# A DeltaNet and SwiGLU kernel whose order of work is planned anew: other durations and another search

## The chip, the cores and the metric

The kernel runs on one core of a Trainium2 chip. The time is the device time of one execution in microseconds; the median of several runs counts. The five engines of the core work side by side, each through its own queue and in order: TensorE (PE; its weight loads are listed apart, as PEld), VectorE (DVE), ScalarE (ACT), GpSimd (POOL) and SyncE (SP), which here only issues DMA transfers. An engine that waits for another holds up everything queued behind the waiting instruction.

## The reference

```python
# deltanet: q, k, v are (4, 8, 768, 48), beta is (4, 8, 768); float32
k_n = k / (norm(k, axis=-1) + 1e-06)
state = zeros((B, H, D, D))
for t in range(S):
    y[:, :, t] = einsum('bhd,bhde->bhe', q[:, :, t], state)
    v_old = einsum('bhde,bhd->bhe', state, k_n[:, :, t])
    state = state + beta_t * einsum('bhd,bhe->bhde', k_n[:, :, t], v[:, :, t] - v_old)
x = y.transpose(0, 2, 1, 3).reshape(3072, 384)
# ffn: d_model 384, d_ff 1536
xn = x / sqrt(mean(x * x) + 1e-06) * rms_g
out = (silu(xn @ w_gate) * (xn @ w_val)) @ w_out
```

The weights arrive as 64-bit floats and are turned into float32 in the kernel.

## The kernel before

**Blocks.** The 768 time steps are cut into 12 blocks of 64. A block c holds all 32 sequences (batch times heads) and yields 256 rows for the FFN. For each block the kernel does four things.

- It reads k, forms its norms (L728 to L735: a Square on ACT, a sum on VectorE, a root on POOL by L731, 1/x on VectorE), turns k (L685, copies L697) and forms the scores of k with itself (L704).
- It inverts the block's triangular matrix. For blocks 0 and 1 (`prep16`) the matrix is taken apart into 16 by 16 pieces: L774/L776, a gather L848, the copy L862, the transpose L865, then pairs of instructions L903 and L909, each pair two columns on, then L924/L926, L929 and the scatter L936. For later blocks (`kscores`, `keep`, `invert`) the scores go through device memory (`dkk`): four writes by SP, two reads into `at`, then L1023, L1048 to L1058 and 15 pairs L1070 and L1076, a POOL copy L1096, and small transfers that spread the result (`dx`, `dxt`, `mt`, `x2bd`, `m1bd`).
- It runs the recurrence (`recur`): products of the state with k and q (L1199, L1210), the corrected values u (L1281 to L1355), q-scores times u (L1317), the update of the state (L1404, L1522), and the norm of the result: L1439, the Square L1445, the root on POOL (L1452 to L1455, in `root`), the scaling L1465, the turn L1483 and, on ACT, L1495, which writes x.
- It runs the FFN on x. Blocks 0 and 1 use plain products (`ffn_plain`: L1558 up, L1565/L1566, L1540 down). Later blocks use a scheme with fewer products (`ffn`: L1651 up, L1661 and L1663 collect, L1667, L1668; `down`: L1708, L1700, L1713, L1717).

**Weights.** The weights come in 18 pieces (`weights`), each read by one DMA of 768 KB into one of three buffers (two early ones elsewhere) and converted by five instructions: ACT L619, then VectorE L607, L610, L615, L639. Later VectorE forms sums of the weights (L1612, L1687).

**q.** For blocks from 2 on, q is read by 16 small transfers (`load`, issued through L487) and turned by one VectorE transpose (`square_turn`, L715).

**What sets the order.** Nothing in the code's order of calls does. Every step is an `Op` with an engine, a planned duration, a priority and the keys it reads and writes; `Plan.run` decides the order of all engines before an instruction is emitted. It does so with a list schedule (`forward`) over the planned durations: an engine takes the op that can start first, then the one with the lowest key. A DMA op takes a planned issue time on SP (`dur`) and then a share of one modelled transfer server (`work`). VectorE's next op may start 0.08 us before an op's planned end (`OVERLAP`). `run` repeats this: first ROUNDS[1] rounds, in which keys are set by a backward pass and shaken by a random generator with seed ROUNDS[0]; then one round for each number in MOVES, which is the seed of one shake that starts from the keys of the round before. The order with the earliest planned end is emitted. Where TensorE is planned to stand idle before 70 us, `fillers` sets dummy products (L1826) into the gap. PSUM's eight banks go from op to op as the plan frees them.

So a changed planned duration moves no instruction by itself. It changes what the plan takes to be early, and by that the order in all five queues.

Of the kernel before, what the change touches and what calls it, by code (L numbers as in the profile page):

```python
# [22 lines left out]
STRETCH = {"PE": 1.5, "ACT": 1.5, "DVE": 1.4, "POOL": 1.2, "SP": 1.0}  # L23
ENGINES = ("PE", "ACT", "DVE", "POOL", "SP")
OVERLAP = {"PE": 0.0, "ACT": 0.1, "DVE": 0.08, "POOL": 0.06, "SP": 0.0}
ROUNDS, MOVES = (8, 3), (8000067, 8000597, 8000948, 8001017, 8002724, 8006360, 8008220, 8019300, 8029128, 8041120, 8046040, 8061420, 8103060, 8171660, 8171980, 8172520, 8176051, 8186548, 8187777, 8188940, 8197021, 8197169, 8200311, 8221546, 8225628, 8270861, 8283640, 8284428, 8285760, 8285870, 8288410, 8295221, 8301729, 8305291, 8310247, 8324080, 8458740, 8499977, 8522895, 8527737, 8540674, 8542770, 8573880, 8576584, 8577340, 8579620, 8580620, 8594840, 8603040, 8637560, 8655411, 8656870, 8664720, 8672920, 8873930, 8885129, 8893086, 8956398, 8960108, 9314698, 9382016, 9442358, 9601943)
BLOCK, ASKED, LACKED = 256, 140, 193
REACT, TURN, LAND = 2.4, 3.45, 2.6
STICK = 1.0
# [315 lines left out]
def kernel(  # L345
# [17 lines left out]
    nc = tc.nc  # L363
# [21 lines left out]
    half = sbt("half", [128, 16])  # L385
# [23 lines left out]
    q2t = q2.rearrange("p x e -> p (x e)").rearrange("p (u g th e) -> p u g th e", u=8, g=2, th=2)  # L409
    q2k = [("q2", i) for i in range(16)]  # L410
# [19 lines left out]
    AK = [("acc", 0), ("acc", 1)]  # L430
# [17 lines left out]
    ms = sbt("ms", [128, 2, 2], 2)  # L448
    rs = sbt("rs", [128, 2], 2)
# [29 lines left out]
    P = Plan()  # L479
    V = lambda n: 0.13 + 0.0011 * n  # L480
    VF = lambda n: 0.13 + 0.0006 * n
    A = lambda n: 0.2 + 0.0008 * n
    G = lambda n: 0.15 + 0.0022 * n

    def dma(dst, src, prio, r=(), w=(), work=0.3, dur=0.5, eng="SP", after=0.0):
        queue = nc.scalar if eng == "ACT" else nc.sync
        op = P.add(eng, dur, lambda: queue.dma_start(out=dst, in_=src), prio, r, w, lat=0.7)  # L487
        op.dma, op.work, op.ready, op.port = True, work, after, False
        return op

# [2 lines left out]
    def due(c, lead):  # L493

        return (64.0 - min(lead, 64.0)) if c == 0 else (90.0 if c == 1 else 152.9 + PERIOD * (c - 2)) - lead
# [156 lines left out]
    def load(c, what):  # L652
        t0 = c * C
        pk, pq, pv = ((-5, 1, 12), (5, 29, 36))[c] if c < 2 else (due(c, 150), due(c, 99), due(c, 70))
        if "q" in what and c > 1:
            for d, eh, g, th in itertools.product(range(2), repeat=4):
                e0, e1 = 32 * eh, min(D, 32 * eh + 32)
                src = q.rearrange("b (yh a) t e -> a t (b yh) e", a=4)[2 * d + g, t0 + 32 * th : t0 + 32 * th + 32, :, e0:e1]
                r0 = 64 * d + 32 * eh
                dma(q2t[r0 : r0 + 32, :, g, th, 0 : e1 - e0], src, pq, w=[q2k[8 * d + 4 * eh + 2 * g + th]], work=0.33 if eh else 0.43, after=due(c, 85))  # L660
        for key, t, src, pr in (("k2", k2[c % NK], k, pk), ("q2", q2, q, pq)):
            for g in range(2):
                if key[0] not in what or key == "q2" and c > 1:
                    continue
                dst = t[64 * g : 64 * g + 64, :, 0:D]
                s = src.rearrange("b (y g) t e -> g t (b y) e", g=2)[g, t0 : t0 + C]
                op = dma(dst, s, pr, w=[(key, c % NK, g)] if key == "k2" else q2k[8 * g : 8 * g + 8], dur=0.7, work=1.18, eng="ACT" if c == 0 and (g or key == "q2") else "SP", after=((0.0, 1.4, 0.0), (5.0, 40, 0.0))[c]["kqv".index(key[0])] if c < 2 else 44.5)
                op.lat += LATE if c == 1 or key == "q2" else 1.2 if c == 0 else 0.0
        if "v" in what and c < 2:
            for g in range(2):  # L670
                s = v.rearrange("b (y g) t e -> g t (b y) e", g=2)[g, t0 : t0 + C]
                dma(vt[64 * g : 64 * g + 64], s, pv, w=[("v", g)], dur=0.7, work=1.18, after=30 if c else 8).lat += LATE
        elif "v" in what:
            for bb in range(2):
                s = v[2 * bb : 2 * bb + 2, :, t0 : t0 + C, :].rearrange("p h t e -> t (p h) e")
                dma(vt[64 * bb : 64 * bb + 64], s, pv, w=[("v", bb)], dur=0.85, work=1.18, after=due(c, 75))
# [106 lines left out]
    def prep16(c):  # L783
        pr = 8.0 if c == 1 else 0.0
        pd = pr + (1 if c else 0)
        pi = (1.0, 45.0)[c]
        i2, ikq = c, c
# [10 lines left out]
        psf = Group()  # L798
# [57 lines left out]
        ab = [("ab", c, n) for n in range(4)]  # L856
        ak = [("acc", c)]
# [15 lines left out]
                nc.scalar.copy(flat(side)[:, L * c : L * c + 33 * 15 + 1 : 33], share())  # L873

        P.add("ACT", 0.6, start, pd, r=["half"], w=ak)
        P.add("ACT", 0.4, start2, pd + 0.5, r=[psf], w=ak, last=psf)
        x, xkeys = x16[c], [("xs", c)]
        diag = a16[c].rearrange("p j t -> p (j t)")[:, 1 : 1 + 34 * 7 + 1 : 34]
        pair = x.rearrange("p i t -> p (i t)")[:, 0:128].rearrange("p (j k) -> p j k", k=L // 2)
# [17 lines left out]
        for j in range(0, L - 2, 2):  # L897
            n, m = j + 2, L - 2 - j

            def step(j=j, n=n, m=m):  # L900
                old, new, lo = (3, 0, 1) if j % 4 else (0, 3, 0)
                cols = slice(L * c + j + 2, L * c + L)
                nc.vector.tensor_tensor(  # L903
                    out=acc[:, 1:3, 0:n, cols].rearrange("p a i t -> p i a t"),
                    in0=sides[old][:, 0:n, j : j + 2, None].to_broadcast([128, n, 2, m]),
                    in1=a16[c][:, None, j : j + 2, j + 2 : L].to_broadcast([128, n, 2, m]),
                    op=ALU.mult,
                )
                nc.vector.tensor_reduce(  # L909
                    out=acc[:, new, 0:n, cols],  # L910
                    in_=acc[:, lo : lo + 3, 0:n, cols].rearrange("p a i t -> p i t a"),
                    axis=AXL.X,
                    op=ALU.add,
                )

            P.add("DVE", 0.47 + 0.0052 * n * m, step, pi, r=ab, w=ak)

        xflat = x.rearrange("p i t -> p (i t)")

# [5 lines left out]
                else:  # L925
                    nc.vector.tensor_copy(out=dst, in_=src)  # L926

        P.add("ACT" if c else "DVE", 0.97 if c else 0.55, spread, pi, r=ak, w=xkeys)
        P.add("DVE", V(256), lambda: nc.vector.transpose(out=turned[1], in_=xflat), pi, r=xkeys, w=["turn1"])  # L929
        psb = Group()  # L930

# [12 lines left out]
        for h in range(2):  # L944
            dst = dg[c][:, 8 * h : 8 * h + 8].rearrange("p x (n m) -> p x n m", n=4)
            src = lambda h=h: psb.t[:, 128 * h : 128 * h + 128].rearrange("p (x m) -> p x m", x=8)[:, :, None].to_broadcast([128, 8, 4, L])
            w = [("dg", c, h)] + (kkall if c else [])
# [62 lines left out]
    def invert(c):  # L1010
        pd = due(c, 110) + 1
# [3 lines left out]
        dkeys = [("dkk", c % 2, g, i) for g in range(2) for i in range(2)]  # L1015
        for par in range(2):
            dma(at_[64 * par : 64 * par + 64].rearrange("p j t -> p (j t)"),
                dk.rearrange("i g x j t -> (i g x) (j t)"), pd, r=dkeys, w=[("at", par)] + [(n_, p_, z) for n_ in ("ab",) for p_ in range(2) for z in range(4)] + [("xs", 0), ("xs", 1)], dur=0.56, work=0.95)
        bt = beta_b[:, c]
        bkeys = [("beta", i) for i in range(8)]  # L1020

# [14 lines left out]
                        bt[rows, par : W : 2],  # L1036
                    )

        P.add("ACT", 1.0, start, pd, r=["half"], w=AK)
        P.add("ACT", 0.9, start2, pd + 0.5, r=bkeys, w=AK)  # L1040


# [22 lines left out]
        for j in range(0, W - 2, 2):  # L1065
            n, m = j // 2 + 1, W - 2 - j

            def step(j=j, n=n, m=m):
                old, new, lo = (3, 0, 1) if j % 4 else (0, 3, 0)
                nc.vector.tensor_tensor(  # L1070
                    out=acc[:, 1:3, 0:n, j + 2 : W].rearrange("p a i t -> p i a t"),
                    in0=acc[:, old, 0:n, j : j + 2, None].to_broadcast([128, n, 2, m]),
                    in1=at_[:, None, j : j + 2, j + 2 : W].to_broadcast([128, n, 2, m]),
                    op=ALU.mult,
                )
                nc.vector.tensor_reduce(  # L1076
                    out=acc[:, new, 0:n, j + 2 : W],
                    in_=acc[:, lo : lo + 3, 0:n, j + 2 : W].rearrange("p a i t -> p i t a"),
                    axis=AXL.X,
                    op=ALU.add,  # L1080
                )

            P.add("DVE", 0.47 + 0.0052 * n * m, step, pi, r=[("at", 0), ("at", 1)], w=AK)

        def spread(dst, op, turn):
            for side in range(2):
# [90 lines left out]
    def recur(c):  # L1177
# [245 lines left out]
        for h in halves:  # L1423
            gy = groups(psy, h)

            if c == 0:
                p = h[0]
                for g in range(2):
                    P.add("ACT", A(192) + 0.15, lambda p=p, g=g: nc.scalar.activation(
                        out=xflat[:, 128 : 320], in_=psy[g, p].t[:, 192 * p : 192 * p + 192], func=ACTF.Square,  # L1430
                        scale=1.0 / math.sqrt(DM), accum_out=ms[i2][:, p, g : g + 1],
                    ), py, r=[psy[g, p]], w=[("x1", 1), ("ms", i2, p)], last=psy[g, p])
# [21 lines left out]
                    nc.gpsimd.tensor_scalar(out=ms[i2][:, cols, 0], in0=ms[i2][:, cols, 0], scalar1=ms[i2][:, h[0], 1:2], scalar2=1e-6, op0=ALU.add, op1=ALU.add)  # L1454
                nc.gpsimd.tensor_tensor(out=rs[i2][:, cols], in0=ms[i2][:, cols, 0], in1=mhalf[:, cols], op=ALU.pow)  # L1455

            P.add("POOL", 1.1, root, py, r=["half"], w=[(k_, i2, p) for p in h for k_ in ("ms", "rs")])
            if c == 0:
                p = h[0]
                P.add("DVE", V(128), lambda p=p: nc.vector.tensor_scalar(  # L1460
# [401 lines left out]
```

## Time and profile before

| what | us |
|---|---|
| runs | 670.78, 671.55, 674.18; median 671.55 |
| profiled execution, its own time | 673.21 |
| its span, first to last instruction | 671.5 |
| TensorE busy | 657.3 (98%) |
| VectorE busy | 577.0 (86%) |
| ACT busy | 298.2 (44%) |
| POOL busy | 88.5 (13%) |
| mean granted clock | 0.994 |

The page cuts the span into 40 slices of 16.8 us; a digit is the busy share of a slice in tenths. Rows of the trace name a line, an engine, an operation and its tiles; where idle time goes before a row, it stands in brackets with what ended it. A helper's line stands for all that call it: L487 is the line of all DMA issues.

| group | count | mean ns |
|---|---|---|
| L1651 PE (up products, blocks 2 to 11) | 2400 records | 276, 277 |
| L1708 PE (down products) | 360 records | 329 |
| L1661 DVE | 180 | 683 |
| L1070 and L1076 DVE (inversion pairs) | 150 and 150 | 351 and 472 |
| at<-dkk, 256 KB, issue to landing | 20 | 3.7 us |
| more<-w_gate, 768 KB, issue to landing | 6 | 7.6 us |

### The profile page before, as it was taken

How to read it: one execution, taken by the hardware profiler on the slowest of the kernel's cores; microseconds unless marked ns; L12 is line 12 of the kernel's file. 1: busy time of each engine (PE TensorE's matmuls, PEld its weight loads, DVE VectorE, ACT ScalarE, POOL GpSimd, SP SyncE). 2: the span in 40 equal slices, each digit the busy share in tenths (PEclk: the TensorE clock that was granted, in tenths of full speed). 3: DMA queues.
4: the chain of work that ended last, by engine and by line, in shares of the span. 5: the costliest groups of instructions: out<-in, count | busy, mean ns of one | idle time of the engine just before them, and what ended most of it. 6: DMA issues, size and time to landing. Idle time of an engine off the chain costs nothing.

```text
span 671.5 us, 23512 instructions
## 1 busy us (share of the span) xinstructions
PE 657.3 (98%) x10070; PEld 608.2 (91%) x10070; DVE 577.0 (86%) x1199; ACT 298.2 (44%) x685; POOL 88.5 (13%) x105
## 2 busy tenths in 40 slices
PE   9899989999999999999999999999999999999997
PEld 6788768787799999999999999999999999999997
DVE  6999889999999998997998898899998798457472
ACT  7554343454235455355345345345345354343241
POOL 4212211050300040040031030030040010000000
PEclk9999979999999999999999999999999999999999
DMA  9483666573325336345347456476346434102100
GB/s 233 125 221 108 135 166 167 91 146 75 48 63 79 63 84 107 57 99 91 54 123 109 76 132 96 82 168 97 48 117 92 84 79 70 26 2 48 24 1 24
DMA packets 261822, 62.31 MB, mean 93 GB/s; under 512 B 248627, under 2 KB 253782, under 8 KB 261718
## 3 DMA queue, kind: packets, MB, share of 16 engines
q1 hardware_dynamic: 258438, 60.02, 45.5%
q8 instruction: 79, 1.29, 0.8%
q10 hardware_dynamic: 3280, 0.79, 0.6%
q14 instruction: 25, 0.20, 0.1%
HBM read 44.25 MB, written 16.52 MB: 91 GB/s over the span
## 4 chain that ended last, share of the span: by engine, by line
PE 79%; DVE 12%; SPq 3%; DMA 2%; issue 2%; ACT 1%; POOL 1%; DVEq 0%; POOLq 0%
PE bank L1651 36%; PE bank L1708 19%; PE bank L1558 7%; PE bank L1540 4%; PE bank L704 3%; PE bank L1199 3%; SPq L487 3%; PE bank L1281 1%; PE bank L1317 1%; DVE tmp L1661 1%; DVE acc L1076 1%; PE bank L685 1%; PE bank L1404 1%; PE bank L1124 1%; DVE acc L1070 1%
## 5 line engine op out<-in xcount | busy, mean ns | idle before, releaser
L1651 PE MATMUL bank<-xf,w_in 128*128 128x128 f32 x1440 | 177.4, 276 | 0.0
L1651 PEld LDWEIGHTS bank<-xf,w_in 128*128 128x128 f32 x1440 | 168.7, 192 | 0.8
L1661 DVE TENSOR_TENSOR tmp<-tmp,bank 128x512 f32<-128x512 f32 x180 | 121.3, 683 | 34.6 <-PE bank L1651 30.2
L1651 PE MATMUL bank<-xf,more 128*128 128x128 f32 x960 | 123.8, 277 | 0.0
L1651 PEld LDWEIGHTS bank<-xf,more 128*128 128x128 f32 x960 | 115.1, 192 | 0.9
L1663 ACT COPY tmp<-bank 128x512 f32<-128x512 f32 x120 | 69.0, 584 | 63.0 <-PE bank L1651 49.4
L1667 ACT ACTIVATE tmp<-tmp 128x256 f32<-128x256 f32 x120 | 50.1, 417 | 93.7 <-DVE tmp L1661 93.2
L1076 DVE TENSOR_REDUCE acc<-acc 128x30 f32<-128x90 f32 (+4 forms) x150 | 70.9, 472 | 5.2
L731 POOL TENSOR_TENSOR knrm<-ksum,half 128x16 f32<-128x16 f32 x12 | 35.5, 2960 | 274.5 <-DVE ksum L730 274.5
L1708 PE MATMUL bank<-wo_sb,hf 128*128 128x192 f32 x360 | 63.8, 329 | 0.0
L1708 PEld LDWEIGHTS bank<-wo_sb,hf 128*128 128x128 f32 x360 | 58.1, 190 | 0.5
L1070 DVE TENSOR_TENSOR acc<-acc,at 128x60 f32<-128x60 f32 (+4 forms) x150 | 52.7, 351 | 2.4
L1668 DVE TENSOR_TENSOR hf<-tmp 128x256 f32<-128x256 f32 x120 | 49.0, 418 | 5.5 <-ACT tmp L1667 4.7
L1540 PE MATMUL bank<-wo_sb,hf 128*128 128x384 f32 x96 | 35.2, 506 | 0.0
L1558 PE MATMUL bank<-xf,w_in 128*128 128x256 f32 x144 | 34.6, 387 | 0.0
L1558 PE MATMUL bank<-xp,w_in 128*128 128x256 f32 x144 | 33.4, 383 | 0.0
L1558 PEld LDWEIGHTS bank<-xp,w_in 128*128 128x128 f32 x144 | 26.8, 190 | 4.6 <-DVE more L1616 0.2
L1558 PEld LDWEIGHTS bank<-xf,w_in 128*128 128x128 f32 x144 | 26.4, 190 | 4.4 <-issue 0.2
L1713 ACT COPY tmp<-bank 128x192 f32<-128x192 f32 x30 | 9.5, 316 | 41.7 <-PE bank L1708 41.2
L1540 PEld LDWEIGHTS bank<-wo_sb,hf 128*128 128x128 f32 x96 | 18.3, 196 | 9.9 <-issue 0.6
L1096 POOL COPY acc<-acc 128x128 f32<-128x128 f32 x40 | 18.8, 500 | 63.1 <-DVE acc L1076 62.8
L1510 DVE TENSOR_TENSOR xf<-xf 128x256 f32<-128x256 f32 (+1 forms) x70 | 24.7, 381 | 2.5 <-ACT xf L1475 1.9
(198 smaller groups left out, 985.8 us busy)
## 6 DMA issues: line engine op xcount, KB each, us to landing
at<-dkk SPq DMA_DIRECT2D x20, 256.0 KB, 3.7
more<-in_moe_w_gate_dram SPq DMA_DIRECT2D x6, 768.0 KB, 7.6
vt<-in_v_dram SPq DMA_DIRECT2D x24, 192.0 KB, 4.0
k<-in_k_dram SPq DMA_DIRECT2D x23, 192.0 KB, 4.2
out_dram<-tmp SPq DMA_DIRECT2D x46, 96.0 KB, 2.2
more<-in_moe_w_val_dram SPq DMA_DIRECT2D x5, 768.0 KB, 8.4
more<-in_moe_w_out_dram SPq DMA_DIRECT2D x5, 768.0 KB, 5.5
dyn<-yn SPq DMA_DIRECT2D x16, 192.0 KB, 2.0
```

The lines of the kernel that those rows point to most:

```text
L731: P.add("POOL", 2.95, lambda: nc.gpsimd.tensor_tensor(out=knrm[i2], in0=ksum[i2], in1=half, op=ALU.pow), pn, r=[("ksum", i2), "half"], w=[ ...
L1070: nc.vector.tensor_tensor(out=acc[:, 1:3, 0:n, j + 2 : W].rearrange("p a i t -> p i a t"), in0=acc[:, old, 0:n, j : j + 2, None].to_broadc ...
L1076: nc.vector.tensor_reduce(out=acc[:, new, 0:n, j + 2 : W], in_=acc[:, lo : lo + 3, 0:n, j + 2 : W].rearrange("p a i t -> p i t a"), axis=A ...
L1510: P.add("DVE", V(128 * n), lambda dst=dst, a=a, b_=b_, op=op: nc.vector.tensor_tensor(out=dst, in0=a, in1=b_, op=op), pxv, r=[("xp", 0)], ...
L1540: nc.tensor.matmul(po[p].t[:, 0:DM], hf[:, spot(f), 128 * p : 128 * p + 128], wo_sb[:, spot(f)], start=(f == f0), stop=(f == f1 - 1), skip ...
L1558: nc.tensor.matmul(ps.t[:, TOK * side : TOK * side + TOK], w_in[:, side, h_, 3 * t + i_, n : n + 128], x_[:, 2 * t : 2 * t + 2].rearrange( ...
L1651: nc.tensor.matmul(g.t[:, 128 * z : 128 * z + 128], fac[:, side, 128 * f : 128 * f + 128], xf[:, xs], start=(begin and z == 0), stop=False ...
L1661: P.add("DVE", V(512), lambda t=t, g=g: nc.vector.tensor_tensor(out=t, in0=t, in1=g.t, op=ALU.add), -1, r=[g], w=[tk], last=g)
L1663: P.add("ACT", A(512), lambda t=t, g=g: nc.scalar.copy(t, g.t), -1, r=[g], w=[tk], last=g)
L1667: P.add("ACT", A(256), lambda t=t: nc.scalar.activation(out=t[:, 0:256], in_=t[:, 0:256], func=ACTF.Silu), -1, w=[tk])
L1668: P.add("DVE", V(256), lambda t=t, f0=f0, p=p: nc.vector.tensor_tensor(out=hf[:, spot(f0) : spot(f0) + 2, 128 * p : 128 * p + 128], in0=t[ ...
L1708: nc.tensor.matmul(g.t[:, 0:192], a_[:, f], b_[:, f], start=(begin and f == 0), stop=(f == 5), skip_group_check=True)
```

## The change

The planner's numbers change, and the seeds of its search. What is computed stays as it is. The lists of seeds are cut.

```diff
-ROUNDS, MOVES = (8, 3), (8000067, 8000597,
+ROUNDS, MOVES = (9, 31), (9000077, 9000084,
...
     def dma(dst, src, prio, r=(), w=(), work=0.3, dur=0.5, eng="SP", after=0.0):
         queue = nc.scalar if eng == "ACT" else nc.sync
-        op = P.add(eng, dur, lambda: queue.dma_start(out=dst, in_=src), prio, r, w, lat=0.7)
+        op = P.add(eng, dur + (0.08 if eng == "SP" else 0.0), lambda: queue.dma_start(out=dst, in_=src), prio, r, w, lat=0.7)
...
# load: the 16 small transfers of q
-work=0.33 if eh else 0.43
+work=0.2 if eh else 0.25
# prep16: start2 (diagonal copies), step (a pair L903/L909), spread
-        P.add("ACT", 0.4, start2, pd + 0.5, r=[psf], w=ak, last=psf)
+        P.add("ACT", 0.3, start2, pd + 0.5, r=[psf], w=ak, last=psf)
-            P.add("DVE", 0.47 + 0.0052 * n * m, step, pi, r=ab, w=ak)
+            P.add("DVE", 0.37 + 0.0052 * n * m, step, pi, r=ab, w=ak)
-        P.add("ACT" if c else "DVE", 0.97 if c else 0.55, spread, pi, r=ak, w=xkeys)
+        P.add("ACT" if c else "DVE", 0.75 if c else 0.42, spread, pi, r=ak, w=xkeys)
# invert: the two reads of dkk into at, the zeroing copy, step (a pair L1070/L1076)
-dur=0.56, work=0.95
+dur=0.56, work=1.3
-        P.add("ACT", 1.0, start, pd, r=["half"], w=AK)
+        P.add("ACT", 0.5, start, pd, r=["half"], w=AK)
-            P.add("DVE", 0.47 + 0.0052 * n * m, step, pi, r=[("at", 0), ("at", 1)], w=AK)
+            P.add("DVE", 0.37 + 0.0052 * n * m, step, pi, r=[("at", 0), ("at", 1)], w=AK)
# recur, block 0: the Square L1429; all blocks: the root on POOL
-                    P.add("ACT", A(192) + 0.15, lambda p=p, g=g: nc.scalar.activation(
+                    P.add("ACT", 0.33, lambda p=p, g=g: nc.scalar.activation(
-            P.add("POOL", 1.1, root, py, r=["half"], w=[(k_, i2, p) for p in h for k_ in ("ms", "rs")])
+            P.add("POOL", 1.1 if c else 0.7, root, py, r=["half"], w=[(k_, i2, p) for p in h for k_ in ("ms", "rs")])
```

MOVES had 63 numbers and has 90; the rounds ahead of them were 3 and are 31.

More of the change, by code (lines that the diff above doesn't have):

```diff
@@ L25 @@
 OVERLAP = {"PE": 0.0, "ACT": 0.1, "DVE": 0.08, "POOL": 0.06, "SP": 0.0}
-ROUNDS, MOVES = (8, 3), (8000067, 8000597, 8000948, 8001017, 8002724, 8006360, 8008220, 8019300, 8029128, 8041120, 8046040, 8061420, 8103060, 8171660, 8171980, 8172520, 8176051, 8186548, 8187777, 8188940, 8197021, 8197169, 8200311, 8221546, 8225628, 8270861, 8283640, 8284428, 8285760, 8285870, 8288410, 8295221, 8301729, 8305291, 8310247, 8324080, 8458740, 8499977, 8522895, 8527737, 8540674, 8542770, 8573880, 8576584, 8577340, 8579620, 8580620, 8594840, 8603040, 8637560, 8655411, 8656870, 8664720, 8672920, 8873930, 8885129, 8893086, 8956398, 8960108, 9314698, 9382016, 9442358, 9601943)
+ROUNDS, MOVES = (9, 31), (9000077, 9000084, 9001020, 9001901, 9001980, 9002345, 9002352, 9005033, 9005360, 9005420, 9007460, 9009163, 9013716, 9013816, 9014640, 9015260, 9031980, 9034094, 9041380, 9054400, 9055600, 9059500, 9072340, 9081389, 9175880, 9175960, 9176640, 9180520, 9200000, 9208667, 9212377, 9286620, 9303250, 9337880, 9350228, 9356206, 9368455, 9401240, 9431340, 9433200, 9487387, 9496993, 9507782, 9520785, 9523803, 9527334, 9600159, 9603986, 9674546, 9699381, 9705015, 9707603, 9708570, 9714080, 9735222, 9844500, 9852292, 9898031, 9898062, 9899208, 9908418, 9952920, 9953455, 10034932, 10036632, 10042493, 10054904, 10068092, 10068412, 10070920, 10072504, 10099741, 10146141, 10146344, 10146905, 10153833, 10157684, 10203905, 10229256, 10250080, 10250921, 10251080, 10252174, 10259126, 10260148, 10262416, 10276413, 10316267, 10316415, 10406558)
 BLOCK, ASKED, LACKED = 256, 140, 193
@@ L659, in load @@
                 r0 = 64 * d + 32 * eh
-                dma(q2t[r0 : r0 + 32, :, g, th, 0 : e1 - e0], src, pq, w=[q2k[8 * d + 4 * eh + 2 * g + th]], work=0.33 if eh else 0.43, after=due(c, 85))
+                dma(q2t[r0 : r0 + 32, :, g, th, 0 : e1 - e0], src, pq, w=[q2k[8 * d + 4 * eh + 2 * g + th]], work=0.2 if eh else 0.25, after=due(c, 85))
         for key, t, src, pr in (("k2", k2[c % NK], k, pk), ("q2", q2, q, pq)):
@@ L1017, in invert @@
             dma(at_[64 * par : 64 * par + 64].rearrange("p j t -> p (j t)"),
-                dk.rearrange("i g x j t -> (i g x) (j t)"), pd, r=dkeys, w=[("at", par)] + [(n_, p_, z) for n_ in ("ab",) for p_ in range(2) for z in range(4)] + [("xs", 0), ("xs", 1)], dur=0.56, work=0.95)
+                dk.rearrange("i g x j t -> (i g x) (j t)"), pd, r=dkeys, w=[("at", par)] + [(n_, p_, z) for n_ in ("ab",) for p_ in range(2) for z in range(4)] + [("xs", 0), ("xs", 1)], dur=0.56, work=1.3)
         bt = beta_b[:, c]
```

## The prediction

> **What bounds the kernel now.** I read the page first, then its stretches, then the time order of VectorE and TensorE around the only hole, and last the order in which the two built programs hold each engine's instructions.
>
> ```profile
> PE   9899989999999999999999999999999999999997
> ...
> DVE  6999889999999998997998898899998798457472
> ...
> PEclk9999979999999999999999999999999999999999
> ```
>
> TensorE is full from slice 7 on and loses time only before about 97 us, where a 7 stands in its clock too. VectorE is as full. The stretches (window: its length, then busy time of each engine, then the granted clock) say which of the two leads:
>
> ```profile
> 12.40:79.90 67.50, 62.58 (x1425) 52.24 (x1424) 65.21 (x138) 35.75 (x73) 10.85 (x10) 1.00 0.61 158
> 79.90:82.55 2.65, 2.65 (x10) 1.57 (x9) 0.00 (x1) 1.12 (x4) 2.56 (x2) 1.00 0.73 146
> 82.70:89.56 6.86, 4.55 (x84) 3.77 (x82) 6.43 (x16) 3.10 (x9) 1.81 (x3) 1.00 1.03 343
> 89.56:96.39 6.83, 5.86 (x74) 4.42 (x75) 6.52 (x14) 2.00 (x4) 1.23 (x1) 0.50 0.68 110
> 107.90:255.00 147.10, 147.10 (x2052) 127.49 (x2051) 141.44 (x283) 65.34 (x154) 22.96 (x24) 1.00 0.48 92
> ```
>
> From 12.4 to 79.9 VectorE leads: end to end its instructions leave 0.1 us. Then it waits 2.65 us for a transfer. TensorE stands still afterwards, and the clock is half for 6.83 us. From 97 us TensorE has no idle and VectorE hardly any up to 255 us: both are bounds. The hole itself:
>
> ```profile
> 79.35 0.55 DVE L1439 TENSOR_TENSOR yn<-yn,bank 128x384 f32<-128x384 f32 x1
> 82.55 1.23 DVE L1023 TENSOR_TENSOR at<-at,beta_b 128x1024 f32<-128x1024 f32 x1 [2.65 <-DMA q<-in_q_dram]
> ```
>
> ```profile
> 86.32 0.93 PE L1404 MATMUL bank<-u,k 64*48 64x48 f32 x64
> 90.53 1.98 PE L704 MATMUL bank<-qt,kt 64*64 64x64 f32 x64 [3.28 <-DVE qt L715]
> 92.44 2.93 PE L1540 MATMUL bank<-wo_sb,hf 128*128 128x384 f32 x4
> 95.16 1.64 PE L685 MATMUL bank<-ident,k 128*128 128x128 f32 x8
> 96.64 2.54 PE L1558 MATMUL bank<-xp,w_in 128*128 128x256 f32 x11
> ```
>
> The q scores (L704) wait for the q transpose on VectorE and stand in front of everything else. At half clock they take 1.98 us (1.09 at 201.6), and the down product 2.93 (1.49 at 125.5). At 96.64 the plain FFN of block 1 (its L1558) begins; from there TensorE is packed. I measure the change by when this instruction can start.
>
> **What the change is.** The programs hold the same instructions but two fillers (19 matmuls of L1826 become 17); only the order differs. The numbers changed are the planner's. Against rows, some come nearer (the diagonal copies 0.4 to 0.3, row 0.26; the first spread 0.55 to 0.42, row 0.40), some go off: the zeroing copy 1.0 to 0.5 (row 1.04), the root 1.1 to 0.7 (0.96), the Square 0.50 to 0.33 (0.45 from start to start), ACT's spread 0.97 to 0.75 (0.98), SP's issue 0.50 to 0.58 (q issues follow every 0.49, a few take 1.2 to 1.6). An inversion step is planned 0.10 shorter; its first pair takes 0.55 from start to start, which is what 0.63 less the planned overlap of 0.08 gave. A planner's time proves nothing here; I follow the new order with the old rows.
>
> **Step 1, to VectorE's start.** The rate products (L804, 0.22 each) now run ahead of the first scores and of L848: +0.25. On ACT the second qt copy (L697, 0.60) stands ahead of the copy L862, which in before ran at 12.04: L865 starts at 13.15 instead of 12.42, +0.7. The fillers hide nothing more.
>
> **Step 2, VectorE to the second L1439.** Both orders put the same 117 instructions between L865 and L1023 (busy sum 71.6). A row that depends on its neighbour starts 0.03 after its end, another 0.08 before it; 41 pairs depend instead of 47: 6 x 0.116 = -0.7. New waits, by laying the rows end to end: 0.4 before the second change L1355 (couple products end at 30.3), 0.2 before L1434, 0.15 before L865 of block 1 (L862 now behind L619 and two Squares), 0.75 before the two L1460 (root on POOL); and 0.9 before L1439, because L1317 stands behind L1252 and an L1558. Sum 2.4 (bounds 0 and 5). So the second L1439 ends at 79.9 + 0.7 - 0.7 + 2.4 = 82.3, and 2.65 of waiting for the transfer is left no room.
>
> **Step 3, the transfer at<-dkk.** On SP two q issues now precede the block writes, and 11 instead of 15 issues stand between those and the second read. SP is first held by the weight load before them (its buffer is freed by an L615 at 66.9 instead of 64.9), so the read is issued at about 78.9, as before (78.91), and lands 3.5 to 3.6 later: 82.5. L1023 starts at 82.7 instead of 82.55. The v reads now follow three weight loads; issued by 84 and landing in 4 to 5 (median of their rows 4.0), they are 15 us ahead of L1246. For block 3 the second read of at<-dkk stands behind a weight load that waits for VectorE until 107; landing at 111.5, it still comes before VectorE gets to L1023, at 114.
>
> **Step 4, the hole.** From L1023 to L1522 the new VectorE order takes 5.4 us for the matrix and three pairs, 0.3 for L1566, then a pair, L734/L735, a pair and both L1522: end at 91.4. TensorE now goes L1404, L1483 (both done at 87.2), L1540 (needs that L1566: 88.5 to 89.8), L1199 of block 2 (needs L1522: 91.45 to 92.55), L685 twice (0.9), L1558 at 93.45. The q scores come after it, and VectorE's transpose is done by then. Before, 96.64 had the same work behind it: **-3.2**.
>
> **Step 5, given back.** VectorE reaches L1076's remaining pairs 1.2 earlier than before, TensorE asks 3.2 earlier, and the new order puts conversions of the weights 8 to 14 us earlier in VectorE's queue. I laid both engines' rows end to end from 98.95 and 93.45: an L1647 group (about 206 us) would start 1.2 us ahead of the L1661 that frees its bank; the same sums on the old order give 0.04, as the trace has no idle there. One conversion asks for a load issued at 107.3; loads of w_gate land after 7.6 (median), and ACT's L619 takes 0.92: 0.6 late. Together **+1.8** (bounds 0 and 4).
>
> **Beyond.** Changes of row mode on TensorE: 117 instead of 116, 0.1 to 0.2 each: nothing. From 255 us VectorE has 12% idle, which covers its lateness. TensorE's last 20 groups are in the same order. Sum: -3.2 + 1.8 = -1.4 on the profiled execution, 673.2 to 671.8. That execution lies 1.7 above its span and 1.7 above the median 671.55; against the median: **670.1**.
>
> **The clock.** Rows: pauses of 0.17 and 3.28 around 87 to 90.5, 2.3 of them before 89.56, halved the clock; 1.2 us at 18.5 did not. The new pauses are 1.2 and 1.7, in different stretches of 6.83 us. The Trainium skill, TensorE: Matmul & The Clock Gate, Part 1, says that the clock falls to half after an idle window of about 3.4 us; by it neither pause costs anything, and the sum stays. No run here shows pauses of this size.
>
> **Rivals.**
> - *The waits of step 2 don't come.* For: they hang on ends of ACT and POOL good to some tenths. Against: `at` is then the limit again; but the load before it moves up too, so L1023 starts near 80.9: 1.8 better, and 0.8 less is given back. -4.0: **667.5**. 0.27.
> - *The clock falls in spite of the pauses' size*, since they add up to 2.9. It costs about 2.9 (5.86 us at half speed); TensorE's being later takes away 1.2 of step 5. +0.3: **671.9**, a change that does not do what its numbers say. 0.13.
> - *Slower: ACT waits for a load ahead of x.* ACT's L619 on a w_gate load now stands ahead of the six L1495 that write x of block 1. The load is issued at about 82; before, it was 81.95 and landed at 89.8. Three loads of 768 KB and two of v now follow each other, 2.75 MB, which at 343 to 233 GB/s (fastest stretch shown, first slice) take 8.0 to 11.8: landing at 90 to 94. At 90, x is ready at 92.6 and nothing is lost; from 91 on, L1558 moves with it. At 94 it starts at 96.7, no gain, the pause of over 4 us halves the clock (2.9), and 0.6 of the load in step 5 stays: +3.5, **675.0**, more if the second load slips too. Against: the same bytes landed in time. 0.17.
> - My forecast has 0.43: -3.3 to +0.6.
>
> **Chances and range.** 0.5% is 3.4 us, about what a measurement of this kernel can tell from no change. Faster by more: 0.27 of the first rival (most of it) and a little of the forecast: 0.28. Slower by more: the slow rival and a tail of the unknown orders past 255 us: 0.20. Within: 0.52. The range runs from 666.8 (past the fast rival) to 675.0 (the slow one).
>
> **What will show it.** In the changed profile: L865 first at about 13.2; L1439 ending near 82.3 and L1023 right after it; L1558 of block 1 (out of xp) at about 93.5; the clock 1.00 between 89 and 97; small idle on PE released by L1661 near 206 and none past 255. L1558 later than 95, a clock of 0.5, or ACT's L619 idle for a w_gate load ahead of L1495 would make me wrong.

## The result, and the profile after

The changed kernel takes 680.97 us (median of 4 runs, 679.88 to 683.07), before 672.46 in the same call: a ratio of 1.013, interval 1.0092 to 1.0169. It is slower; the forecast was 670.1 with a range to 675.0. The profiled execution took 679.88 (span 678.2), 6.7 more than that of before; it is the shortest of the four, so its rows show 6.7 of the 8.5 us by which the medians differ.

Page of the changed kernel, its span in slices:

```profile
PE   8879989999999999999899999999999999999997
...
DVE  5989999999998998897789899998998699457473
...
PEclk9999999999999999999899999999999999999999
```

The 7 at slice 6 in the clock is gone. An 8 has come at slice 20 in TensorE's row and in its clock, and VectorE has a 7, 7, 8 there, from 305 to 356 us. First the place that the forecast was made for, as rows in order of time (start, duration, engine), VectorE and then TensorE:

```profile
82.09 1.02 DVE L1439 TENSOR_TENSOR yn<-yn,bank 128x384 f32<-128x384 f32 x2 [0.83 <-PE bank L1317]
83.02 1.22 DVE L1023 TENSOR_TENSOR at<-at,beta_b 128x1024 f32<-128x1024 f32 x1
```

```profile
85.98 0.94 PE L1404 MATMUL bank<-u,k 64*48 64x48 f32 x64
...
88.78 1.56 PE L1540 MATMUL bank<-wo_sb,hf 128*128 128x384 f32 x4 [0.72 <-DVE hf L1566]
91.20 1.50 PE L1199 MATMUL bank<-state,kt 48*64 48x48 f32 x64 [0.87 <-DVE state L1522]
...
93.56 2.76 PE L1558 MATMUL bank<-xp,w_in 128*128 128x256 f32 x12
```

L1558 of block 1 starts at 93.56 (forecast 93.45, before 96.64). Up to here 3.1 us are gained. From it to the end of the span the kernel takes 678.2 - 93.56 = 584.6 us, before 671.5 - 96.64 = 574.9: **9.8 us are lost behind**. The rows of TensorE past 97 us with idle ahead of them, and the windows (length, busy of each engine, clock, DMA share, GB/s):

```profile
146.44 1.05 PE L1483 MATMUL bank<-ident,yn 128*128 128x128 f32 x6 [0.61 <-DVE hf L1566]
...
331.50 0.64 PE L1152 MATMUL bank<-x2bd,yn 128*32 128x128 f32 x16 [1.95 <-ACT yn L1134]
...
496.78 1.15 PE L1317 MATMUL bank<-u,pt 64*64 64x48 f32 x64 [0.97 <-DVE u L1351]
504.74 2.05 PE L1651 MATMUL bank<-xf,more 128*128 128x128 f32 x16 [0.53 <-DVE tmp L1661]
```

```profile
87.28:94.11 6.83, 5.11 (x85) 3.57 (x84) 6.50 (x17) 5.00 (x13) 1.48 (x1) 1.00 1.00 242
107.90:255.00 147.10, 146.25 (x2056) 126.87 (x2055) 139.96 (x283) 62.89 (x151) 22.66 (x24) 1.00 0.46 89
326.23:333.06 6.83, 4.88 (x132) 4.29 (x132) 5.33 (x10) 2.40 (x7) 0.00 (x0) 1.00 0.42 52
333.06:339.88 6.82, 6.82 (x99) 6.73 (x92) 6.51 (x20) 2.56 (x6) 0.00 (x0) 0.50 0.50 86
```

Seven pauses past 97 us (0.61, 0.22, 1.95, 0.97, 0.53, 0.15, 0.29) make 4.7; the stretch at half clock costs 3.4. The other 1.7 have no one place: TensorE's busy time behind L1558 is 575.54 against 570.39 in before, 1.7 more than the half clock accounts for. Before had one pause of this size between 97 and 660 us:

```profile
577.80 0.25 PE L1199 MATMUL bank<-state,qt 48*64 48x48 f32 x1 [0.44 <-issue]
```

When it was lost can be estimated by counting each record of TensorE at its mean step in before. By that the changed kernel is 1.5 us ahead of before at 255 us, 0.9 ahead at 326, 3.9 late at 340, 5.4 late at 506 and 6.7 late at the end.

Where the longest pause comes from is seen on SP and VectorE:

```profile
312.49 0.63 SPq L487 DMA_DIRECT2D yn<-dyn  x1
313.94 2.80 SPq L487 DMA_DIRECT2D dkk<-kk  x4
316.79 0.60 SPq L487 DMA_DIRECT2D yn<-dyn  x1
...
323.70 0.59 SPq L487 DMA_DIRECT2D yn<-dyn  x1
```

```profile
326.82 1.23 DVE L1023 TENSOR_TENSOR at<-at,beta_b 128x1024 f32<-128x1024 f32 x1 [2.71 <-DMA at<-dkk]
328.85 0.98 DVE L1473 STREAM_TRANSPOSE xf<-yn 128x768 f32<-128x768 f32 x1 [0.80 <-DMA yn<-dyn]
```

The four reads that bring x of block 5 back are spread over 11 us by other issues (298.8 to 306.9 in before). Its transpose L1473 stands behind L1023, which waits 2.71 for `at`, and then waits 0.80 more for the last of the four reads. On ACT three L1475 wait for L1473 and stand ahead of L1134, which starts at 331.08; TensorE's L1152 waits for L1134.

**One thing about the clock has to be known for all that follows.** The mean granted clock differs from execution to execution of one kernel. In 63 runs of before it was 1.000 in 4 (670.9 on average, 669.1 to 673.0), 0.997 in 32 (672.3), 0.995 in 10 (674.5), 0.994 in 9 (673.2): a line through all gives 0.48 us for each 0.001, and 670.9 at full clock. It is a rough line, as 0.995 and 0.994 show. The mean also counts the end of each execution: in before's profile the clock is 0.5 from 669.83, after TensorE's last matmul (667.55), which costs nothing. The profiled execution of before, at 0.994, was one with much loss.

**What the planner itself counts.** `run` computes an end for each of its passes and keeps the best. That count is no chip time, but it is there before anything runs. In before the 3 rounds reach 679.60; the first shake ends later (691.48), and from there the ends fall almost from shake to shake, to 666.27 at the last of the 63. In the changed kernel the best of 121 passes is number 31, the last plain round, at **672.29**; each of the 90 shakes ends later (the last four near 688). By the planner's own count the new order is 6.0 longer.

But the two ends are counted with different durations. Run through `forward` with the other kernel's durations, each order fixed, the order of before ends at 682.83 by the new durations (the new order: 672.29), and the new order at 684.55 by the old ones (before: 666.27). So each set of durations prefers its own order by more than 10 us, and by the new durations the count has the sign wrong. That each count by its own durations had the sign right is no proof that the planner can tell.

### The profile page after: what moved, and what is told of

Same layout as the page of the kernel before. It is cut to its first block, busy times and chain, and to the rows that moved or that the text cites. A ratio compares the mean times of both kernels' runs of the same rounds, so it can differ in the third digit from the quotient of the medians.

```text
span 678.2 us, 23514 instructions
## 1 busy us (share of the span) xinstructions
PE 657.0 (97%) x10066; PEld 608.5 (90%) x10066; DVE 574.8 (85%) x1199; ACT 297.2 (44%) x685; POOL 87.1 (13%) x105
## 4 chain that ended last, share of the span: by engine, by line
PE 59%; DVE 24%; SPq 5%; DMA 5%; issue 3%; ACT 2%; POOL 1%; DVEq 0%; ACTq 0%; POOLq 0%
PE bank L1651 31%; PE bank L1708 15%; SPq L487 5%; DVE acc L1076 4%; DVE acc L1070 3%; DVE tmp L1661 3%; PE bank L1558 2%; PE bank L1199 2%; PE bank L704 2%; PE bank L1540 2%; DMA vt<-in_v_dram 1%; DMA q<-in_q_dram 1%; PE bank L1281 1%; PE bank L1317 1%; DVE hf L1668 1%
## 5 line engine op out<-in xcount | busy, mean ns | idle before, releaser
L1651 PE MATMUL bank<-xf,w_in 128*128 128x128 f32 x1440 | 180.7, 278 | 0.1
L1651 PEld LDWEIGHTS bank<-xf,w_in 128*128 128x128 f32 x1440 | 171.1, 193 | 2.3 <-DVE tmp L1661 0.2
L1661 DVE TENSOR_TENSOR tmp<-tmp,bank 128x512 f32<-128x512 f32 x180 | 119.9, 679 | 35.3 <-PE bank L1651 27.4
L1651 PE MATMUL bank<-xf,more 128*128 128x128 f32 x960 | 126.1, 279 | 0.9 <-DVE tmp L1661 0.9
L1651 PEld LDWEIGHTS bank<-xf,more 128*128 128x128 f32 x960 | 116.2, 193 | 2.7 <-DVE tmp L1661 1.5
L1558 PE MATMUL bank<-xf,w_in 128*128 128x256 f32 x144 | 34.1, 384 | 0.3 <-DVE xf L1489 0.3
L1558 PE MATMUL bank<-xp,w_in 128*128 128x256 f32 x144 | 32.5, 381 | 0.0
L1558 PEld LDWEIGHTS bank<-xf,w_in 128*128 128x128 f32 x144 | 26.7, 190 | 5.4 <-issue 0.4
L1558 PEld LDWEIGHTS bank<-xp,w_in 128*128 128x128 f32 x144 | 27.0, 190 | 4.3
```

Of the source, the lines that this page charges most:

```text
L1558: nc.tensor.matmul(ps.t[:, TOK * side : TOK * side + TOK], w_in[:, side, h_, 3 * t + i_, n : n + 128], x_[:, 2 * t : 2 * t + 2].rearrange( ...
L1651: nc.tensor.matmul(g.t[:, 128 * z : 128 * z + 128], fac[:, side, 128 * f : 128 * f + 128], xf[:, xs], start=(begin and z == 0), stop=False ...
L1661: P.add("DVE", V(512), lambda t=t, g=g: nc.vector.tensor_tensor(out=t, in0=t, in1=g.t, op=ALU.add), -1, r=[g], w=[tk], last=g)
```

## The experiments

Fourteen of the sixteen kernels change the order and nothing else (the planner's fillers on TensorE vary by a few matmuls); two add two matmuls. "Fixed list" means that the order of the 2837 operations is written out. "Planned" is the planner's best end, counted with the kernel's own planned durations. Each ratio is to the runs of before in the same call.

| run | order | planned | measured | ratio to before, interval |
|---|---|---|---|---|
| before (in its calls 672.2 to 673.3) | own list | 666.27 | 672.3 | 1 |
| changed kernel | | 672.29 | 680.97 | 1.0130, 1.0092-1.0169 |
| new_list | old durations, new ROUNDS and MOVES | 676.59 | 681.64 | 1.0156, 1.0109-1.0204 |
| old_list | new durations, old ROUNDS and MOVES | 683.95 | 690.18 | 1.0252, 1.0235-1.0268 |
| root_only | before, one duration changed | 679.92 | 688.87 | 1.0231, 1.0199-1.0263 |
| no_list | before without shakes | 679.60 | 689.37 | 1.0242, 1.0211-1.0273 |
| half_list | before, 32 of 63 shakes | 670.89 | 675.82 | 1.0042, 1.0024-1.0061 |
| fit_after | new durations, list fitted anew | 667.20 | 680.14 | 1.0102, 1.0087-1.0118 |
| fit_after2 | the same from another start | 667.72 | 676.15 | 1.0060, 1.0037-1.0082 |
| fit_before | old durations, list fitted anew | 669.48 | 681.22 | 1.0116, 1.0087-1.0144 |
| first98 | new order to 98 us, then old | | 672.76 | 1.0012, 0.9993-1.0031 |
| rest92 | old order to 92 us, then new | | 679.38 | 1.0104, 1.0069-1.0139 |
| fill5, fill6 | matmuls into a pause | | 682.45, 679.39 | 1.0153, 1.0124-1.0183; 1.0112, 1.0087-1.0136 |
| x_first | x reads together | | 678.61 | 1.0094, 1.0075-1.0112 |
| x_first_2, x_dve | and a second place | | 680.93, 679.54 | 1.0146, 1.0122-1.0170; 1.0101, 1.0071-1.0130 |
| hole2 | before, one hole filled | | 671.08 | 0.9982, 0.9971-0.9993 |

### Where the loss is: first98 and rest92

```diff
-ROUNDS, MOVES = (9, 31), (9000077, ...)
+ORDER = (the new order's operations planned before 98 us, then the others as in before)
```

> The changed kernel's order for everything that its plan starts before 98 us (past the first L1558 of block 1 out of xp), then the order of before for all that is left, written out as a fixed list of operations; no instruction is added or left out. Theory A (the early stage of the new order is a gain of 3.1 us, and the whole loss, some 10 us, comes from the order past 98): L1558 of xp starts near 93.6 as in the changed kernel, VectorE gives back up to 1.8 afterwards, the two bad places of the changed kernel (329 and 488 to 505 us) are gone: 669.5 to 671.5, or 1 to 3 below before. Theory B (what the early stage saves on TensorE is taken back soon, because VectorE is no earlier there than before, 83.0 against 82.55): 672 to 674, no gain against before. Theory C (the planned durations themselves, not the place, cost): cannot be told here, as only the order differs.

672.76, no gain: theory B. L1558 of xp starts at 96.62 here, though the order is the new one, since the clock was half twice on the way:

```profile
21.88:25.29 3.41, 3.35 (x63) 3.38 (x65) 3.38 (x7) 0.59 (x1) 1.75 (x1) 0.50 0.02 7
38.95:42.36 3.41, 3.41 (x15) 3.21 (x15) 2.33 (x9) 1.05 (x3) 0.00 (x0) 0.50 1.05 393
```

VectorE reaches L1023 at 86.09 instead of 83.02. The early part has its own pauses (1.86 at 18, 2.80 at 36), so it trades one chance of half clock for another. The two runs at 0.999 took 671.1 and 671.2, the four of before at full clock 670.9 on average: so few runs show no gain of the new early stage even undisturbed.

> The reverse: the order of before up to the first L1558 of block 1 out of xp (planned at 92 us), then the changed kernel's order. Theory A: the hole and the half clock of before are back (+3.1) and all of the loss past 98 is there: 681 + 3 = 684, up to 685. Theory B (the early part of the new order makes VectorE or the transfers late and so causes the later stalls): the stalls at 329 and 488 to 505 us are smaller or gone, 673 to 677.

679.38, 7.1 above before: below what theory A said (684), above what B said (673 to 677). With first98 this places the loss in the order past 93 us. That it is not 684 has a reason in the trace: TensorE is 3.1 later than in the changed kernel up to 325 us, its pause before L1152 is 1.67 instead of 1.95, and no half clock follows; at the end it is 1.3 later.

### What makes the new order bad: durations or search

> All durations of before, with only ROUNDS and MOVES of the changed kernel. Theory A (what the list of shakes finds sets the time: with before's own list the planner's best order ends at 666.27 by its own count and the span was 671.5, with the new list none of the 90 shakes betters the plain rounds and the best ends at 676.59): span 676.59 + 5 to 6 = 682, time 683 to 684, at least as slow as the changed kernel. Rival (the new durations cost, the list is harmless): 671 to 674, as before.

Theory A. With the same rounds and shakes, old and new durations run alike (681.64 and 680.97); by the intervals a difference of up to some 4 us either way could hide in that, so this says only that the new durations as such cost nothing that shows.

> All the planned durations of the change, with ROUNDS and MOVES of before; planned end 683.95. Theory A: 683.95 + 5 to 7 = 689 to 691. Rival (the new list is what costs, the durations are a gain): below 680.

Theory A. The list that takes before to 666.27 does little for the new durations (best pass 12 of 66), and the run is the slowest of all.

```diff
-            P.add("POOL", 1.1, root, ...
+            P.add("POOL", 1.1 if c else 0.7, root, ...
```

> Before with one edit of the change alone: the planned time of the root on POOL for block 0 (L1457, 1.1 to 0.7), which concerns two of 2837 operations. By the planner's count its best order ends at 679.92 with the list of before, 13.6 later than before. Theory A (the list fits one set of durations only, any edit undoes it): 685 to 687. Rival (an edit of two small operations moves a few orders near 40 us): 670 to 674.

Theory A, and a little beyond: one planned duration of two operations on POOL, no instruction changed, and the kernel is 2.3% slower. By the planner's count each of the ten edits does this by itself (planned ends of 679.92 to 686.81 with before's list); only this one was run.

> Before with its 63 shakes left out: all its durations, its 3 plain rounds; planned end 679.60 (with the list 666.27). Theory J (what sets before apart is what its list does to the order: each shake that shortens the plan also shortens the run): 685 to 688, some 14 over before. Theory K (the list as such is worth little, orders of plain rounds run at 680 to 682, as the changed kernel's, planned at 672.3, and that with the old durations and the new list, planned at 676.6): 680 to 683.

689.37, theory J, worse than it said. TensorE has waits in it that before's profile does not have:

```profile
PE bank L1540 <- DVE hf L1566: 7.2, 2, 6.7
PE bank L1708 <- DVE xp L1700: 6.0, 3, 4.2
```

> Before with the first 32 of its 63 shakes: planned end 670.89. Theory J (along this list the run follows the plan): planned end + 6, 676 to 678. Theory K (the planned end says little below 675, as the two fitted lists showed with 667.2 and 669.5 planned and 680 and 681 measured, and before is one lucky order among many): 679 to 682.

675.82, theory J again (planned 670.89). Along before's own list, at three points of it, the time follows the planned end: 679.60, 670.89, 666.27 planned, 689.4, 675.8, 672.3 measured.

> All the planned durations of the change, its 31 rounds, but another list of 17 shakes, each of which was kept because the plan ended earlier with it: its best order ends at 667.20 by the planner's count (changed kernel 672.29, before 666.27). Theory A (the change costs because its list of shakes does nothing for these durations, and the order is that of a plain round): time = planned end + 5 to 7, as for before (666.27 and 672.24) and for the run with the new list and the old durations (676.59 and 681.64): 672 to 674, that is 7 to 9 under the changed kernel and level with before. Rival D (the new durations themselves mislead the planner, whatever its search): 678 to 682, like the changed kernel.

```diff
-ROUNDS, MOVES = (9, 31), (9000077, ... 90 numbers)
+ROUNDS, MOVES = (9, 31), (23000544, ... 17 numbers)
```

680.14: theory A fails here. The plan is 5.1 shorter than the changed kernel's and the run is 0.8 shorter (1.9 by the ratios; the intervals overlap). The clock is no excuse (0.996 to 0.999).

> All the planned durations of before, with other rounds and a list of 28 shakes found in the same way and with about the same number of tries as in the run before this one: planned end 669.48. Theory A: time = planned end + 5 to 7: 674.5 to 676.5, a little slower than before (its own list got to 666.27). Rival D (the old durations are the better ones, so a list that suits them gives a faster kernel at the same planned end): 672 or less, and at least 2 under the fitted kernel with the new durations once the planned ends are taken off.

681.22: theory A fails here too, and D with it.

> The change's durations with 28 other rounds and a list of 23 shakes kept for a shorter plan, from another start: planned end 667.72. Theory J': planned end + 6 to 7, 674 to 675, and the first fitted list (667.20, 680.1) was bad luck. Theory K: 679 to 682 again, as stalls that the plan doesn't foresee (VectorE's L1661 behind transfers and behind inversion pairs) make up what the plan saves.

676.15: neither figure, nearer to J'. So the first fitted list was partly bad luck; a plan fitted for length still loses 8 to 13 us when it runs, before's 6. Over all ten kernels of the table with a planned end, measured less planned is 4.9 to 12.9, mean 8.3, and the two go together with a correlation of 0.90. Much of that comes from the four planned above 676: among the six planned below 673 it is 0.51.

### The single places: the pause at 331, the waits at 496, the hole at 87

> The changed kernel with two matmuls of 128x512 (identity by identity, as the fillers of L1826, some 1.8 us) put on TensorE directly ahead of L1152 of block 5, where it stood idle for 1.95 us at 329.55 and the clock was half from 333.06 to 339.88; they write the bank that L1152 overwrites. Theory A (the pause itself makes the clock fall, which costs 3.3 us behind it): no stretch at 0.5 near 333, time 681.0 - 3.3 = 677.7. Rival (the clock falls for another reason, such as the small tiles of L1124, L1152 and L1199 around it): still half, 681 or a little over. Second rival (the clock stays, but what is gained is lost again to VectorE within the next 100 us): clock 1.00 and time 680 to 681.

This missed its place: block 5's L1152 stands at 287, where TensorE had no pause; the fillers held it up by 1.7 there. Yet at 331 the pause shrank from 1.95 to 1.28, no half clock followed, and TensorE had those 1.7 us back and 2 more (0.9 of it was lost again by 350).

> The changed kernel with two matmuls of 128x512 (1.8 us) in the pause ahead of L1152 at 331.5 (block 6; the first try had put them ahead of block 5's, at 287, where TensorE had no pause). Only the clock can gain: theory A (the pause makes the clock fall): no half clock near 333, 681 - 3.3 = 677.7 or a little more. Rival: TensorE's gain of 3.3 is lost again within 100 us, because VectorE is no earlier: 680 to 681.

```diff
                     if with_merge:
+                        if c == 6:
+                            for _ in range(2):
+                                nc.tensor.matmul(ps2.t[:, 0:512]..., ident, ident[:, None, :].to_broadcast([128, 4, 128]))
                         merge2_products(c, ps2)
```

Theory A for the place: no half clock at 333, and TensorE, 3.7 us late until then from half clock at 22 and 39, is only 0.4 late behind it. 3.3 are gained there and kept (0.6 late at the end). The median falls only by 1.6 (the intervals overlap), between theory A and the rival; the mean clocks of these runs (0.992 to 0.997) say that half clock is in all of them elsewhere.

```profile
333.17 1.98 PE L1232 MATMUL bank<-ident 128*128 128x512 f32 x4
335.09 0.64 PE L1152 MATMUL bank<-x2bd,yn 128*32 128x128 f32 x16
```

> The changed kernel's order as a fixed list, with three reads of yn<-dyn (block 4's x, issued at 316.8, 319.8 and 323.7 between other transfers) put directly behind the first one at 312.5, ahead of the four writes dkk<-kk that wait for ACT, and with VectorE's L1473 ahead of its L1023, where VectorE stood idle for 2.7 us waiting for at<-dkk. Nothing else moves on any engine; banks may get other numbers. Theory E (the pause of 1.95 us ahead of L1152 at 331.5 and the half clock behind it come from these late reads): L1473 near 325 instead of 328.9, pause 0.6 or less, clock 1.00 from 326 to 340: 681 - 1.4 - 3.3 = 676 to 677. Rival F (VectorE is the bound here, so the pause only moves to its next wait): 679.5 to 681.

```diff
 ORDER: yn<-dyn, yn<-dyn, yn<-dyn, yn<-dyn, then dkk<-kk x4 (SP); L1473, then L1023 (VectorE)
```

(The x is block 5's, not block 4's.) 678.61, 2.4 below the changed kernel (the intervals overlap), between theory E (676 to 677) and rival F (679.5 to 681). At the place theory E is right:

```profile
316.87 3.36 SPq L487 DMA_DIRECT2D yn<-dyn  x4
```

```profile
334.52 0.64 PE L1152 MATMUL bank<-x2bd,yn 128*32 128x128 f32 x16 [0.51 <-ACT yn L1134]
```

The pause is 0.51 instead of 1.95, the clock stays, TensorE goes from 4.46 late (half clock at 37 and 92 in this execution) to 0.15 early, and loses 0.75 of it again by 350.

> The same, and two groups of L1651 put ahead of L1317 of a later block on TensorE, where it stood idle for 0.97 us at 496 waiting for VectorE's L1351. Theory E: another 1.0 us off the run before this one: 675 to 676. Rival F (VectorE bounds this place too): the idle moves to the next L1651 behind an L1661, no gain over x_first.

680.93: worse than rival F said, 2.3 above x_first and clear of its interval. Of the two groups that the list puts ahead, one (8 records) stands ahead of L1317 in the trace. It needs a bank that VectorE frees later; the pause of 0.97 becomes one of 2.34, with half clock behind it:

```profile
496.25 1.86 PE L1651 MATMUL bank<-xf,more 128*128 128x128 f32 x8 [2.34 <-DVE tmp L1661]
```

> The run x_first with two more moves on VectorE alone: one L1661 and the L1351 that TensorE's L1317 waits for at 496 go ahead of two inversion pairs that need nobody (1.0 us each). Theory E (each of the changed order's waits past 97 us can be taken away where it stands): TensorE's 0.97 us at 496 goes, and the time is 1 below x_first: 677 to 678. Rival F (VectorE is full there, so the pairs' lateness comes back as the next wait, at 504 or at the next use of their result): 678 to 680.

Rival F: 679.54. In the trace L1661 and L1351 stand ahead of one inversion pair, not two. The wait of L1317 (1.00 in x_first) is gone and comes back in two places, one of which had 0.52 in x_first:

```profile
499.94 1.16 PE L1651 MATMUL bank<-xf,more 128*128 128x128 f32 x8 [0.52 <-DVE tmp L1661]
506.51 2.05 PE L1651 MATMUL bank<-xf,more 128*128 128x128 f32 x16 [0.95 <-DVE tmp L1661]
```

Here VectorE has inversion pairs without a break, and moving one piece ahead delays another.

> The order of before as a fixed list, with one change: the first two L1558 groups of block 1 (2.6 us, ready at 87.8) ahead of the q scores (L704), which wait for VectorE until 90.5; that fills the only hole and keeps the clock. Theory G, that of the prediction (TensorE has no other idle, so what the hole costs is the gain): 2.6 us plus what half clock the runs of before have (0 to 3 us): 668 to 670, 2.5 to 4 below before. Rival H (VectorE is packed from 97 to 255 and no earlier, so it takes the gain back; only the half clock is saved): 671 to 672, 1 below before.

```diff
 ORDER (TensorE): L1404, L704 of q, L1540, ..., L1558, L1558
              ->  L1404, L1558, L1558, L704 of q, L1540, ...
```

671.08, 0.18% below before (interval 0.07% to 0.29%) and the fastest of all. Rival H.

```profile
86.56 0.94 PE L1404 MATMUL bank<-u,k 64*48 64x48 f32 x64
87.43 2.86 PE L1558 MATMUL bank<-xp,w_in 128*128 128x256 f32 x12
90.22 1.16 PE L704 MATMUL bank<-qt,kt 64*64 64x64 f32 x64
```

The hole is full, and 9 of 12 runs have a clock of 1.000 (4 of 63 in before). But the mean of those 9 is 670.9, and that of the 4 of before is 670.9 too, if only on four runs. In the hole's stead TensorE waits three times behind it, the third time 0.34 us at 104.2:

```profile
94.47 1.16 PE L704 MATMUL bank<-kt 64*64 64x64 f32 x64 [0.73 <-ACT kt L697]
...
98.73 1.56 PE L1558 MATMUL bank<-xp,w_in 128*128 128x256 f32 x6 [0.69 <-DVE hf L1566]
```

The other engines are no earlier and take back what TensorE gained; by the medians the half clock is all that filling the hole saves.

## Why the prediction was wrong

**Step 1, the start, right.** L865 at 12.90 (forecast 13.15, before 12.42).

**Steps 2 and 3, VectorE and the transfer, right.** The second L1439 ends at 83.1 with its last wait 0.83 (forecast 82.3 and 0.9), the second read is issued at 78.87, L1023 starts at 83.02 (forecast 82.7), and nothing waits for the transfer. (The 0.1 us that VectorE is said to leave from 12.4 to 79.9 is its longest pause between two instructions; the window shows 2.3 us of idle.)

**Step 4, the hole, right in the profile and mis-sized as a gain.** -3.1 measured against -3.2. But most of the 3.2 was the 6.83 us at half clock of that one execution, priced as if every run had it; half of the runs show a mean of 0.997, about one piece of 3.41. hole2 fills the same hole and gains 1.2 at the median; first98 takes this early stage as it is and gains nothing. The sum should have held about -1, or 0 with the early pauses.

**Step 5, given back, near in size up to 255 us, by luck in part.** It was sized +1.8 with bounds of 0 and 4, and the stretch past 255 us was taken apart from it. At 255 us TensorE is still 1.5 ahead (estimate above): 1.6 given back. But neither place it was priced for shows: the L1647/L1651 group near 206 has no pause in the trace, and VectorE does not wait between 107.8 and 122, where the late load was to hold it. TensorE idles 0.85 of 147.10 us up to 255 instead, at 146 and 246.

**"Beyond", the step that failed.** Past 255 us the sum has nothing. "From 255 us VectorE has 12% idle, which covers its lateness" and "the last 20 groups are in the same order" were taken as proof that nothing happens between. I followed both engines' rows from one place and took the rest of the order as given. The trace shows some 8 of the 9.8 us lost past 255 (1.5 ahead there, 6.7 late at the end): pauses at 331, 497 and 505 and the half clock at 333. An idle share of 12% did not help: at 326 VectorE itself waited 2.7 us for `at`, and at 496 it was full.

**The clock.** The rival was named for 89 to 97 us, where it did not happen (1.72 idle in the stretch from 87.28). It happened at 333, behind a pause of 1.95. The Trainium skill, TensorE: Matmul & The Clock Gate, Part 1, gives an idle window of about 3.4 us for it. The measurement decides, and pauses of 1.86 (first98, at 18) to 2.80 (first98, at 36) were enough. The same section of the Trainium skill calls the window free-running, so that one kernel meets it at another phase in each run. By that the runs agree: with the same order up to there, the changed kernel's profile has pauses of 1.85 and 2.69 at these two places and full clock behind both. In half_list even a pause of 3.21 at 87 left the clock at 1.00.

**The rivals.** None had the mechanism. The chances held "a tail of the unknown orders past 255 us", but with no price, and the range ended at 675.0. The slower one (ACT's L619 ahead of L1495) did not come: L1495 follows L619 at 88.17, and L1558 waits for nobody.

**The cause as far as it is shown.** The loss lies in the order past 93 us: rest92, with that order alone, loses 7.1, and first98, with the early part alone, nothing clear of noise. Its largest single piece is the pause at 331 with its half clock, 5.4 us in the profile; without it the median is 2.4 lower, though the intervals overlap.

**What is only argued** is why this order is worse. The 90 new shakes do nothing for the plan, so the kernel runs a plain round, and before without its shakes does run long (no_list, 689.37). But the fitted lists, whose shakes shorten the plan to that of before, still run 0.6% to 1.2% over before, so the idle list is not the whole of it. Nor is it shown that the new durations do not mislead the planner: they rate the new order above that of before, and the chip does not. Against it stands that fit_before, fitted with the old durations, runs no better than the two with the new.

**What stays open** is why orders fitted anew to a planned 667 to 669 lose 2 to 8 us more against their plan than before and half_list (6.0 and 4.9) do. fit_after's trace has five waits behind VectorE's L1661, 3.0 us together, fit_before's two, 1.3 us, and neither a single cause.

## What to carry to other kernels

Where a planner sets the order, a changed cost is not a local edit: the whole order is drawn again, and a list of moves tuned to the old costs is void, as one duration of two operations showed (+2.3%). Rows laid end to end over the first part of a new order say nothing of the rest; an idle share is no reason to price the rest at nothing. Look at the planner's own end before and after as a warning, no more: two ends compare only when counted with the same durations, and here even those preferred their own order. Price a pause that halves the clock by how often the runs have it, not by the one execution that was profiled, and take TensorE's gain in front of a full VectorE for nothing until a run shows it.

## What the runs showed of the hardware that was not expected

- The granted clock falls to 0.5 in pieces of 3.41 or 6.83 us. It did so behind pauses of 1.95 us (at 331), 1.86 (at 18 in first98) and the first 2.3 of one of 3.28 (at 87 in before), and not behind one of 3.21 (at 87 in half_list). Where it falls differs between traces that have the same order up to there.
- The clock's mean explains a third of the variance between runs of before: 0.48 us for each 0.001.
- A clock lost in the first 50 us, where VectorE leads, cost 1.2 to 1.6 us for a piece of 3.41 up to 44 us (fill5 and fill6 against the changed kernel, the same order there; in fill6 the two pieces had grown to 3.8 together by 92); one lost at 333, where TensorE leads, costs 3.3 for 6.83.
